# A three-stage attention and expert kernel: reductions through a transposing DMA, a capped work list, and scales from ScalarE's sums

## The chip, the cores and the metric

The kernel runs on one core of one Trainium2 chip. The metric is the device time of one execution in microseconds. Before the change it is 1496.46 us, the median of three runs (1494.01 to 1498.49). Engines are named as in the profile: PE is TensorE (PEld its weight loads), DVE is VectorE, ACT is ScalarE, POOL is GpSimd, and SP issues most DMAs.

## The reference

Three computations follow each other. The first is attention over 2 batches, 8 heads, 768 positions and 64 channels, in which a query sees only keys of its own cluster. The second is a network on its output, the third a mixture of 8 experts.

```python
# x: 1536 x 512, from the attention
h = x @ w_in                       # 512 x 2048
g = h * clip(h + 3.0, 0.0, 6.0) / 6.0
x = g @ w_out                      # 2048 x 512
logits = x @ w_gate;  logits = logits - logits.max()
P = exp(logits)
for _ in range(8):                 # balance rows and columns
    P /= P.sum(1) + 1e-09;  P /= P.sum(0) + 1e-09;  P *= N / E
out = 0
for e in range(8):
    out += P[:, e:e+1] * (maximum(x @ w1[e], 0.0) @ w2[e])    # 512 x 1024, 1024 x 512
```

## The kernel before

All matrix products work on pairs of float16 matrices: a float32 operand is scaled by a power of two and split into a high and a low part (names `ws`, `w_s`, `wop`, `xop`, `hh` and `hl`), and three products make one. The power of two comes from the largest absolute value of the operand. So for each operand that is split there is a maximum over a whole tile, and after it one scale.

Such a maximum is taken in two ways. `top_steps` writes each partition's maximum into a column of `pad` (DVE, L101), turns that column into rows by a matmul with the identity (PE, L77), reduces the rows on DVE (L82), and brings the result to all partitions by another matmul (PE, L87). `top_turned` (from L118) does without PE: DVE reduces, copies the maximum to a 128x128 block (L123), SP issues a transposing DMA (L124), and DVE reduces the turned block (L128). After both, `scale_of` makes the scale in four small operations of DVE (L140 to L149). Before the change `top_turned` serves the experts' weights from w1 of expert 1 and w2 of expert 0 on.

The work around the change has four parts. Every engine does its instructions in the order in which the program lists them, so an instruction that waits holds up all behind it on its engine.

1. Layer 1 of the first half of the network (`l1_mm`, L914 to L916) is 24 steps of twelve matmuls: 8 columns of hidden units, 3 blocks of 512 tokens. ACT and DVE make the activation from each step's result (L1231, L1232, L1238). Beside it DVE and ACT decode the second weights of this half (`w_1_c`, from L179) and split them (L271, L274).
2. Layer 2 of this half (L1260) is 24 steps of twelve matmuls, with ACT taking out each block (L1268). Beside it the weights of the second half are decoded: w_in (w1_0 of the task list, tiles `w_0_c`), the gate's weights (wg), and w_out (w1_1, tiles `w_1_c`). The order of a decode is load (L179), ACT L185, DVE L190 to L208, and a maximum by DVE L260 or by a sum of ACT L257.
3. The loop over the second half has 26 steps: layer 1 of a step, its activation, and layer 2 (L1260) of the step before the last one. After each block of 8 steps DVE adds four tiles of result into `acc` (L1270). At the end of each step `run_todo` runs some of a work list, `todo`: w1 of expert 0 in four pairs (`pair`, with POOL L1372 to L1378, ACT L1389 and DVE L1393, through one buffer `cmb`), the maximum of w2 of expert 0, and the splitting of the network's output, `x2_tasks`, for each finished block (x2_0, x2_1; x2_2 comes with the first units). A task's first number is its weight in the list; `run_todo` spends in a step the sum of weights divided by the steps left.
4. The experts are 96 units of 7 slots. Each slot has a product (L1660) and two groups of the second product (L1602), with ACT and DVE between them (L1561, L1566, L1665 to L1671). Weights of the next expert are loaded (L1417 for w2), their maxima taken (DVE L1422) and split (ACT L1389 and L1432) in between.

Of the kernel before, what the change touches and what calls it, by code (L numbers as in the profile page):

```python
# [9 lines left out]
F16 = mybir.dt.float16  # L10
# [22 lines left out]
def attention_moe_kernel(  # L33
# [82 lines left out]
    def top_turned(cols, name, then):  # L116

        pb = pad.bitcast(BF16)  # L118

        def a():  # L120
            m1 = small.tile([P, 1], F32, tag="w_m1", name=f"{name}_m1")
            nc.vector.tensor_reduce(m1, cols(), axis=AX.X, op=ALU.max)
            nc.vector.tensor_copy(pb[:, 0:P], m1.bitcast(BF16)[:, 1:2].to_broadcast([P, P]))  # L123
            nc.sync.dma_start_transpose(out=pad.bitcast(F16)[:, P:2 * P], in_=pad.bitcast(F16)[:, 0:P])  # L124

        def b():
            m = small.tile([P, 1], F32, tag="w_m", name=f"{name}_m")
            nc.vector.tensor_reduce(m, pb[:, P:2 * P], axis=AX.X, op=ALU.max)  # L128
            then(m)

        return [a, b]
# [86 lines left out]
    def weight_tasks(n, m, pool, raw=None):  # L218
# [70 lines left out]
        parts = []  # L289
        for i in range(NP):  # L290
            parts += [(0.05, lambda i=i: hi(i)), (0.2, lambda i=i: lo_pool(i)) if (n, m) == (1, 0) else (0.7, lambda i=i: lo(i))]
        scale = top_steps(lambda: d["mx"], 1, nm, room1, scale1)
        return start, [("m", piece(i)) for i in range(NP)], scale, parts

    def pipeline(pieces, depth):
# [704 lines left out]

    todo = []

    def run_todo(left):

        due = sum(c for c, _ in todo) / left
        while todo and (due > 0.01 or left <= 1):
            c, f = todo.pop(0)
            due -= c
            f()
            if f in far and left > 1:  # L1010
                return
# [3 lines left out]
    def turns(n):  # L1015
        def pause():
            pass

        far.append(pause)
        return [(0.0, pause)] * n  # L1020
# [16 lines left out]
    def gate_weights():  # L1037
        raw = mp.tile([P, KD, NE], F32, name="wg_raw")
        mx = small.tile([P, 1], F32, name="wg_mx")

        def g0():
            nc.sync.dma_start(raw, w_gate.rearrange("(c p) e -> p c e", p=P))

        def g1():
            nc.vector.tensor_reduce(mx, raw, axis=AX.XY, op=ALU.max, apply_absolute_value=True)

        def g1s(m):
            wgs["s"], wgs["i"] = scale_of(m, 1, 2, "wg", const)

        def g2():  # L1050
            nc.scalar.activation(wg[:, 0], raw, AF.Copy, scale=wgs["s"])
            nc.vector.scalar_tensor_tensor(
                out=wg[:, 1], in0=raw, scalar=wgs["s"], in1=wg[:, 0], op0=ALU.mult, op1=ALU.subtract)

        return [(0.05, g0), (0.3, g1)] + hops(top_steps(lambda: mx, 0, "wg", room1, g1s)) + [(0.3, g2)]

    cfac = {}

# [16 lines left out]
    xTf = xT.rearrange("p z c t n -> p (z c t n)")  # L1075
    XOP = 2 * 7 * 2 * XT

    def x2_tasks(bk, room):
        d = {}

        def q(h, g):
# [71 lines left out]
        vs = {"b12": q12, B11: q11, B21: q21, B22: q22, T1: T1, T2: T2, T3: T3, T4: T4}  # L1153
        t = [(0.9, lambda h=h, g=g: amax(h, g)) for h in range(2) for g in range(2)]
        t += [(0.1, diff(T1, q12, q11))]
        first, top, t = t, top_steps(lambda: d["mx"], 0, f"x2_{bk}", room, sc1), []
        order = [B11, B21, T1, B22, T2, "b12", T4, T3]
        for i, o in enumerate(order):
            t.append((0.1, hi(o, vs[o])))
# [11 lines left out]
    def balance_tasks():  # L1171
# [34 lines left out]
                o, i = (x.rearrange("p (g t) e -> p g t e", g=B)[:, :, NX * bk:NX * bk + NX, :] for x in (px, pr))  # L1206
                nc.vector.tensor_scalar(out=o, in0=i, scalar1=invx[bk][:, 0:1], scalar2=None, op0=ALU.mult)

        return top_steps(lambda: lg, 0, "lg", spare, m1) + [f for n in range(8) for f in (total, lambda n=n: col(n < 7))]

    coef = {}

# [38 lines left out]
    def layer2(n, blk, f):  # L1251
# [18 lines left out]
                nc.vector.scalar_tensor_tensor(  # L1270
                    out=o, in0=v, scalar=cfac[1], in1=o, op0=ALU.mult, op1=ALU.add)
        if n == 1:
            first, top, rest, logits = x2_tasks(blk, room1 if blk < NBK - 1 else spare)
            if blk < NBK - 1:
                todo[0:0] = first + hops(top, 1) + rest + turns(2) + [(0.5, lambda: logits(red_bank[-1]))]
            else:
                x2_last.extend((first, top, rest, logits))

# [62 lines left out]
    def expert_w1(e):  # L1341
# [22 lines left out]
        def pair(i):  # L1364
# [26 lines left out]
            def lo(k):  # L1391
# [6 lines left out]

        return (
            [lambda i=i: load(i) for i in range(4)], [lambda i=i: amax(i) for i in range(4)],  # L1400
            top_turned(lambda: d["mx"], f"w{n}_0", scale1) if e else top_steps(
                lambda: d["mx"], 1, f"w{n}_0", room1, scale1),
            [pair(i) for i in range(4)])

    def expert_w2(e):
# [13 lines left out]
                w2[e].rearrange("(a f p) n -> a p f n", a=2, p=P)[a, :, :, 256 * b:256 * b + 256])  # L1419

        def amax(j):
            nc.vector.tensor_reduce(  # L1422
                d["mx"][:, j:j + 1], rawbuf[:, j], axis=AX.X, op=ALU.max, apply_absolute_value=True)

        def scale1(m1):
            d["s"], wsc[n, 1] = scale_of(m1, 1, 3, "ws1", small, bufs=4)

        def src(k):
            return (R11, R21, R11, d.get("t1"), R12, R22, R21)[k]
# [40 lines left out]
    for s in range(len(steps) + LAG2):  # L1470
# [8 lines left out]
        if s == 4:  # L1479
            load, mx, sc, prs = expert_w1(0)  # L1480
            todo += [(0.05, f) for f in load] + [(6.0, nothing)] + [(1.2, f) for f in mx] + hops(sc)
            for c0, c1, hi, lo in prs:
                todo += [(0.1, c0), (0.1, c1), (0.1, hi[0]), (0.9, lambda hi=hi, lo=lo: (lo[0](), hi[1]()))]
                todo += [(0.4, lambda hi=hi, lo=lo: (lo[1](), hi[2]())), (1.3, lo[2])]
            load, mx, sc, hi, lo, ts = first_w2
            todo += [(0.05, f) for f in load] + [(6.0, nothing)] + [(1.2, f) for f in mx] + hops(sc)
        near = [(NB * f + blk) % 4 for _, blk, f in steps[max(0, s - 1):s + 2]]
        red_bank.append(BANKS[4 + next(b for b in range(4) if b not in near)])

        run_todo(max(2 if s + 1 < len(steps) + LAG2 else 1, len(steps) - 5 - s))  # L1490
    hctx.close()
    wctx.close()

# [218 lines left out]
    first, top, rest, logits = x2_last  # L1712
    for n, (_, f) in enumerate(first):
        at2(n, f)
    at_hops(5, top)
    for n, (_, f) in enumerate(rest):
        at2(9 + n, f)
    at2(9 + len(rest) + 2, lambda: logits(1))
# [59 lines left out]
```

## Time and profile before

| | us |
|---|---|
| median of three runs | 1496.46 (1494.01 to 1498.49) |
| the profiled execution | 1495.44, its span 1493.5 |
| busy in the span: PE, DVE, ACT, POOL | 1368.7, 1238.9, 873.1, 818.7 |
| layer 2 of the second half begins | 439.49 |
| the experts' main part | 690 to 1460 |

A busy time is the sum over an engine's instructions in the span. PE is the fullest one, with 92%, and its waits are gathered in a few places. The stretches that matter here are 338 to 353 (layer 1), 431 to 440 (the seam between the halves), 440 to 577 (the loop) and 577 to 690 (the first units).

### The profile page before, as it was taken

How to read it: one execution, taken by the hardware profiler on the slowest of the kernel's cores; microseconds unless marked ns; L12 is line 12 of the kernel's file. 1: busy time of each engine (PE TensorE's matmuls, PEld its weight loads, DVE VectorE, ACT ScalarE, POOL GpSimd, SP SyncE). 2: the span in 40 equal slices, each digit the busy share in tenths (PEclk: the TensorE clock that was granted, in tenths of full speed). 3: DMA queues.
4: the chain of work that ended last, by engine and by line, in shares of the span. 5: the costliest groups of instructions: out<-in, count | busy, mean ns of one | idle time of the engine just before them, and what ended most of it. 6: DMA issues, size and time to landing. Idle time of an engine off the chain costs nothing.

```text
span 1493.5 us, 31114 instructions
## 1 busy us (share of the span) xinstructions
PE 1368.7 (92%) x12361; PEld 1064.7 (71%) x12361; DVE 1238.9 (83%) x2154; ACT 873.1 (58%) x1636; POOL 818.7 (55%) x865
## 2 busy tenths in 40 slices
PE   2888788797999969799999999999999999999998
PEld 1556566543444425687888888888888888888887
DVE  7889998875775567999889989989989989989854
ACT  3568767566372444656667656656656656655642
POOL 1579888944121123845746646655655655655631
PEclk9789889998999989999999999999999999999999
DMA  8575743241420000101111011011011111111001
GB/s 222 140 159 102 153 83 70 60 127 39 127 88 27 29 28 2 43 16 43 31 45 48 26 44 58 16 44 58 23 37 58 31 31 57 31 30 58 9 29 50
DMA packets 148753, 88.62 MB, mean 59 GB/s; under 512 B 82048, under 2 KB 144512, under 8 KB 148608
## 3 DMA queue, kind: packets, MB, share of 16 engines
q1 hardware_dynamic: 148608, 86.64, 22.2%
q8 instruction: 96, 1.57, 0.4%
q14 instruction: 49, 0.40, 0.1%
HBM read 64.01 MB, written 3.15 MB: 45 GB/s over the span
## 4 chain that ended last, share of the span: by engine, by line
PE 69%; DVE 18%; ACT 4%; issue 4%; POOL 1%; DMA 1%; SPq 0%; DVEq 0%; ACTq 0%; POOLq 0%
PE o_X L1602 16%; PE X L1660 16%; PE o_Z L1602 8%; PE Z L1660 8%; PE Y L1660 4%; PE o_Y L1602 4%; DVE pmt L677 3%; PE l L1260 3%; PE l L914 2%; PE l L916 2%; PE l L915 2%; PE pmt L674 1%; DVE g L1566 1%; DVE raw L208 1%; DVE w_t L206 1%
## 5 line engine op out<-in xcount | busy, mean ns | idle before, releaser
L1660 PEld LDWEIGHTS <-wop 128*128 128x128 f16 x4032 | 395.5, 98 | 64.9 <-issue 17.9
L1602 PEld LDWEIGHTS <-g 128*128 128x128 f16 x4032 | 395.1, 98 | 46.2 <-DVE g L1566 0.3
L1602 PE MATMUL o_X<-ws,g 128*128 128x256 f16 x2304 | 312.1, 273 | 0.0
L1570 POOL TENSOR_TENSOR xT<-xT 128x256 f32<-128x256 f32 x96 | 77.6, 809 | 283.4 <-ACT xT L1671 283.4
L744 POOL TENSOR_TENSOR El<-E,Eh 128x384 f16<-128x384 f32 x192 | 189.8, 1017 | 72.6 <-DVE Eh L740 40.6
L1566 DVE TENSOR_TENSOR g<-xT,g 128x512 f16<-128x512 f32 (+1 forms) x288 | 225.5, 783 | 0.2
L1660 PE MATMUL X<-xop,wop 128*128 128x256 f16 x1536 | 210.2, 274 | 8.2 <-DVE xT L1668 4.7
L1561 ACT CAST g<-xT 128x512 f16<-128x512 f32 (+1 forms) x288 | 157.8, 548 | 2.8 <-POOL xT L1574 2.8
L1602 PE MATMUL o_Z<-ws,g 128*128 128x256 f16 x1152 | 157.2, 274 | 0.0
L1665 ACT COPY xT<-X 128x256 f32<-128x256 f32 x192 | 71.3, 372 | 146.4 <-PE X L1660 146.4
L731 ACT ACTIVATE E<-pS,esc 128x768 f32<-128x768 f32 x96 | 86.2, 900 | 65.5 <-PE pS L727 42.7
L1671 ACT ACTIVATE xT<-xT 128x256 f32<-128x256 f32 x192 | 100.1, 521 | 27.3 <-DVE xT L1668 27.0
L1671 ACT ACTIVATE xT<-X 128x256 f32<-128x256 f32 x96 | 36.8, 383 | 134.1 <-PE X L1660 133.9
L1660 PE MATMUL Z<-xop,wop 128*128 128x256 f16 x768 | 105.4, 274 | 5.4 <-ACT xT L1665 3.8
L1660 PE MATMUL X<-xT,wop 128*128 128x256 f16 x768 | 105.4, 274 | 0.8 <-DVE xT L1668 0.8
L1630 DVE SCALAR_TENSOR_TENSOR acc<-o_X,coef,acc 128x256 f32<-128x256 f32 x168 | 73.0, 475 | 28.1 <-PE o_X L1602 28.1
L677 DVE TENSOR_REDUCE pmt<-pmt 128x1 f32<-128x768 f32 x84 | 80.5, 959 | 18.9 <-PE pmt L674 18.3
L1574 POOL TENSOR_TENSOR xT<-xT 128x256 f32<-128x256 f32 x96 | 93.1, 970 | 0.0
L674 PE MATMUL pmt<-kA,qA 80*128 80x384 f16 x184 | 51.7, 367 | 43.2 <-DVE pmt L677 13.8
L1575 POOL TENSOR_TENSOR sb<-xT 128x256 f32<-128x256 f32 x96 | 86.8, 904 | 7.5
L1571 POOL TENSOR_TENSOR sb<-xT 128x256 f32<-128x256 f32 x96 | 82.5, 860 | 5.0 <-ACT xT L1665 4.3
L1435 DVE SCALAR_TENSOR_TENSOR ws<-raw,ws_s,ws 128x1024 f16<-128x1024 f32 x48 | 80.8, 1684 | 0.9 <-ACT ws L1432 0.9
(304 smaller groups left out, 2900.7 us busy)
## 6 DMA issues: line engine op xcount, KB each, us to landing
raw<-in_moe_w_dram SPq DMA_DIRECT2D x64, 256.0 KB, 3.2
raw<-in_moe_w_dram SPq DMA_DIRECT2D x32, 512.0 KB, 3.5
w_c<-in_moe_w_out_dram SPq DMA_DIRECT2D x16, 512.0 KB, 3.3
w00x<-in_moe_w_in_dram SPq DMA_DIRECT2D x8, 512.0 KB, 5.2
w00f<-in_moe_w_in_dram SPq DMA_DIRECT2D x8, 512.0 KB, 4.4
w_c<-in_moe_w_in_dram SPq DMA_DIRECT2D x8, 512.0 KB, 3.9
qraw<-in_q_dram SPq DMA_DIRECT2D x8, 384.0 KB, 3.9
kraw<-in_k_dram SPq DMA_DIRECT2D x8, 384.0 KB, 4.8
```

The source lines that it names most:

```text
L677: nc.vector.tensor_reduce(nmx[i][:, j:j + 1], ps[:, :, 0:N2], axis=AX.XY, op=ALU.max, negate=True)
L731: nc.scalar.activation(E, ps[:, :, 0:N2], AF.Exp, scale=d["esc"][:, 0:1])
L744: nc.gpsimd.tensor_tensor(out=El[:, g], in0=E[:, g], in1=Eh[:, g], op=ALU.subtract)
L1435: nc.vector.scalar_tensor_tensor(out=w2op[k][:, 1], in0=src(k), scalar=d["s"][:, 0:1], in1=w2op[k][:, 0], op0=ALU.mult, op1=ALU.subtract)
L1561: nc.scalar.copy(t[:, 0] if n == 2 else t[:, 0, 0], src)
L1566: nc.vector.tensor_tensor(o, d[g], x, op=ALU.subtract)
L1571: nc.gpsimd.tensor_tensor(out=d["sb"][:, 0], in0=q3, in1=q2, op=ALU.subtract)
L1574: nc.gpsimd.tensor_tensor(out=sa[:, 0], in0=sa[:, 1], in1=q3, op=ALU.subtract)
L1575: nc.gpsimd.tensor_tensor(out=d["sb"][:, 1], in0=q1, in1=sa[:, 0], op=ALU.subtract)
L1602: nc.tensor.matmul(o, lhsT=x, rhs=r, start=first and z == 0, stop=last and z == 2, skip_group_check=True)
L1660: nc.tensor.matmul(o[n][:, 0:XT], lhsT=l, rhs=r, start=(first and c == 0 and z == 0), stop=(c == 1 and z == 2), skip_group_check=True)
L1671: nc.scalar.activation(q, q if src is None else src, AF.Relu)
```

## The change

It has three parts. First, nine maxima go from `top_steps` to `top_turned`: the weights w0_1, w1_0, wg and w1_1 of the network, w1 of expert 0, the three blocks x2 and the logits lg. Second, the last loop's work list is spent with a cap of 3.2 per step, only the last step empties it, x2 tasks go to its end in place of its front, and the last two parts of a pair are a turn apart. Third, from expert 1 on the scale of w2 comes from a sum of absolute values on ACT and a target of 13, in place of a maximum on DVE and a target of 3.

```diff
@@ top_turned
         def a():
             m1 = small.tile([P, 1], F32, tag="w_m1", name=f"{name}_m1")
-            nc.vector.tensor_reduce(m1, cols(), axis=AX.X, op=ALU.max)
+            x = cols()
+            nc.vector.tensor_reduce(m1, x, axis=AX.X if len(x.shape) == 2 else AX.XY, op=ALU.max)
...
@@ weight_tasks (w0_1, w1_0, w1_1)
-        scale = top_steps(lambda: d["mx"], 1, nm, room1, scale1)
+        scale = top_turned(lambda: d["mx"], nm, scale1)
...
-    def run_todo(left):
-
-        due = sum(c for c, _ in todo) / left
+    def run_todo(left, most=1e9):
+
+        due = min(sum(c for c, _ in todo) / left, most) if left > 1 else 0
         while todo and (due > 0.01 or left <= 1):
             c, f = todo.pop(0)
             due -= c
...
-        return [(0.05, g0), (0.3, g1)] + hops(top_steps(lambda: mx, 0, "wg", room1, g1s)) + [(0.3, g2)]
+        return [(0.05, g0), (0.3, g1)] + hops(top_turned(lambda: mx, "wg", g1s)) + [(0.3, g2)]
...
-        first, top, t = t, top_steps(lambda: d["mx"], 0, f"x2_{bk}", room, sc1), []
+        first, top, t = t, top_turned(lambda: d["mx"], f"x2_{bk}", sc1), []
...
-        return top_steps(lambda: lg, 0, "lg", spare, m1) + [f for n in range(8) for f in (total, lambda n=n: col(n < 7))]
+        return top_turned(lambda: lg, "lg", m1) + [idle] + [f for n in range(8) for f in (total, lambda n=n: col(n < 7))]
...
             if blk < NBK - 1:
-                todo[0:0] = first + hops(top, 1) + rest + turns(2) + [(0.5, lambda: logits(red_bank[-1]))]
+                todo.extend(first + hops(top, 1) + rest + turns(2) + [(0.5, lambda: logits(red_bank[-1]))])
...
-            top_turned(lambda: d["mx"], f"w{n}_0", scale1) if e else top_steps(
-                lambda: d["mx"], 1, f"w{n}_0", room1, scale1),
+            top_turned(lambda: d["mx"], f"w{n}_0", scale1),
...
         def amax(j):
-            nc.vector.tensor_reduce(
-                d["mx"][:, j:j + 1], rawbuf[:, j], axis=AX.X, op=ALU.max, apply_absolute_value=True)
+            if e == 0:
+                nc.vector.tensor_reduce(
+                    d["mx"][:, j:j + 1], rawbuf[:, j], axis=AX.X, op=ALU.max, apply_absolute_value=True)
+                return
+            junk = epool.tile([P, 1024], F16, tag="ev", name=f"w{n}_1_t{j}", bufs=3)
+            nc.scalar.activation(junk, rawbuf[:, j], AF.Abs, accum_out=d["mx"][:, j:j + 1])
 
         def scale1(m1):
-            d["s"], wsc[n, 1] = scale_of(m1, 1, 3, "ws1", small, bufs=4)
+            d["s"], wsc[n, 1] = scale_of(m1, 1, 13 if e else 3, "ws1", small, bufs=4)
...
-                todo += [(0.4, lambda hi=hi, lo=lo: (lo[1](), hi[2]())), (1.3, lo[2])]
+                todo += [(0.4, lo[1])] + turns(1) + [(0.1, hi[2]), (1.3, lo[2])]
...
-        run_todo(max(2 if s + 1 < len(steps) + LAG2 else 1, len(steps) - 5 - s))
+        run_todo(2 if s + 1 < len(steps) + LAG2 else 1, 3.2)
...
-    at_hops(5, top)
+    at_hops(5, top, 4)
```

After the change most lines have a number higher by one (L915 is L914 of before, L1394 is L1393, L125 is L124); from the new sum on it is four.

The first place is PE in layer 1 of the first half, at the maximum of w0_1. Before:

```order
L916 MATMUL l_0_2_5_5310<-xT,w_0_s 128x512
L77 MATMUL red_5330<-ident,pad 128x128
L87 MATMUL red_5334<-ident,w_1_r 128x1
L914 LDWEIGHTS w_0_s
L914 MATMUL l_0_0_6_5342<-xT,w_0_s 128x512
```

At the same place after:

```order
L917 LDWEIGHTS w_0_s
L917 MATMUL l_0_2_5_5313<-xT,w_0_s 128x512
L915 LDWEIGHTS w_0_s
L915 MATMUL l_0_0_6_5341<-xT,w_0_s 128x512
L916 LDWEIGHTS w_0_s
```

The two matmuls of the maximum are gone from PE's row; the layer's matmuls follow each other.

The second place is SP's queue before the loads of the second half's w_out (`w_1_c`), with the gate's weights ahead of them. Before:

```order
L179 DMA w_0_c_5593<-in_moe_w_in_dram 128x1024
L179 DMA w_0_c_5614<-in_moe_w_in_dram 128x1024
L1042 DMA wg_raw<-in_moe_w_gate_dram 128x4x8
L179 DMA w_1_c_5752<-in_moe_w_out_dram 128x1024
L179 DMA w_1_c_5754<-in_moe_w_out_dram 128x1024
L179 DMA w_1_c_5756<-in_moe_w_out_dram 128x1024
```

After:

```order
L180 DMA w_0_c_5592<-in_moe_w_in_dram 128x1024
L180 DMA w_0_c_5613<-in_moe_w_in_dram 128x1024
L1043 DMA wg_raw<-in_moe_w_gate_dram 128x4x8
L125 DMA_TRANSPOSE pad<-pad 128x128 x2
L180 DMA w_1_c_5749<-in_moe_w_out_dram 128x1024
L180 DMA w_1_c_5751<-in_moe_w_out_dram 128x1024
```

Two transposes, those of w1_0 and wg, now stand ahead of the eight loads.

The third place is DVE in the last loop, ahead of the evacuation of a block (`acc`), with the pairs of expert 0's w1 (`wop`, their last part from `cmb`). Before, at the second block:

```order
L1393 SCALAR_TENSOR_TENSOR wop_2_6678<-raw,ws_s,wop_2_6678 128x512
L1232 SCALAR_TENSOR_TENSOR u_2_0_6695<-u_2_0_6695,l_1_2_0_6682 128x512
L1239 TENSOR_TENSOR hl_2_0_6699<-u_2_0_6695,hh_2_0_6698 128x512
L1393 SCALAR_TENSOR_TENSOR wop_2_6678<-raw,ws_s,wop_2_6678 128x256
L1393 SCALAR_TENSOR_TENSOR wop_2_6678<-cmb_2_6673,ws_s,wop_2_6678 128x1024
L1393 SCALAR_TENSOR_TENSOR wop_3_6722<-raw,ws_s,wop_3_6722 128x512
L1393 SCALAR_TENSOR_TENSOR wop_3_6722<-raw,ws_s,wop_3_6722 128x256
L1393 SCALAR_TENSOR_TENSOR wop_3_6722<-cmb_3_6717,ws_s,wop_3_6722 128x1024
L1232 SCALAR_TENSOR_TENSOR u_2_1_6747<-u_2_1_6747,l_1_2_1_6734 128x512
L1239 TENSOR_TENSOR hl_2_1_6751<-u_2_1_6747,hh_2_1_6750 128x512
L1270 SCALAR_TENSOR_TENSOR acc<-l_1_1_0_6407,cfac_6023,acc 128x2x256
```

After, at the first block, where the pairs now stand:

```order
L1394 SCALAR_TENSOR_TENSOR wop_0_6303<-raw,ws_s,wop_0_6303 128x512
L1394 SCALAR_TENSOR_TENSOR wop_0_6303<-raw,ws_s,wop_0_6303 128x256
L1233 SCALAR_TENSOR_TENSOR u_1_0_6321<-u_1_0_6321,l_1_1_0_6308 128x512
L1240 TENSOR_TENSOR hl_1_0_6325<-u_1_0_6321,hh_1_0_6324 128x512
L1394 SCALAR_TENSOR_TENSOR wop_0_6303<-cmb_0_6298,ws_s,wop_0_6303 128x1024
L1394 SCALAR_TENSOR_TENSOR wop_1_6347<-raw,ws_s,wop_1_6347 128x512
L1394 SCALAR_TENSOR_TENSOR wop_1_6347<-raw,ws_s,wop_1_6347 128x256
L1233 SCALAR_TENSOR_TENSOR u_1_1_6365<-u_1_1_6365,l_1_1_1_6352 128x512
L1240 TENSOR_TENSOR hl_1_1_6369<-u_1_1_6365,hh_1_1_6368 128x512
L1271 SCALAR_TENSOR_TENSOR acc<-l_1_0_0_6089,cfac_6019,acc 128x2x256
```

Two pairs' `cmb` rows stood between two u before; now there is at most one, and u and hl stand between a pair's raw rows and its `cmb` row.

## Rows read from the trace of the kernel before

**Rows 1.** Busy time by stretch: stretch, length, engines, PE clock, DMA.

```profile
338.00:353.00 15.00, 6.99 (x22) 2.78 (x21) 7.33 (x17) 8.00 (x15) 8.02 (x6) 0.66 0.23 70
353.00:369.50 16.50, 16.50 (x78) 7.51 (x77) 8.68 (x14) 12.93 (x20) 7.04 (x6) 1.00 0.00 1
439.50:576.60 137.10, 123.35 (x614) 56.06 (x613) 84.90 (x137) 53.63 (x81) 25.46 (x25) 0.95 0.10 31
525.00:541.00 16.00, 5.15 (x15) 1.74 (x13) 11.07 (x17) 5.27 (x7) 7.23 (x7) 0.68 0.19 66
577.00:690.00 113.00, 95.11 (x834) 79.95 (x832) 105.25 (x200) 66.57 (x140) 70.84 (x68) 0.96 0.10 30
690.00:1460.00 770.00, 767.18 (x7019) 686.63 (x7018) 679.71 (x1147) 467.29 (x979) 452.55 (x488) 1.00 0.12 38
```

**Rows 2.** Timeline, PE at 343 us: start, duration, idle before and releaser.

```profile
343.94 0.45 PE L77 MATMUL red<-ident,pad 128*128 128x128 f32 x1 [4.47 <-DVE pad L101]
347.93 0.59 PE L87 MATMUL red<-ident,w_r 128*128 128x1 f32 x2 [3.54 <-DVE w_r L82]
348.38 0.59 PE L914 MATMUL l<-xT,w_s 128*128 128x512 f16 x1
352.17 0.58 PE L914 MATMUL l<-xT,w_s 128*128 128x512 f16 x1
```

**Rows 3.** Tile pad, steps of top_turned: count, min/median/max ns; the transpose's landing.

```profile
L123 DVE COPY pad<-w_m x15: 226/568/570, 568.7 to 1379.7; 128x128 bf16<-128x128 bf16 x15
L124 SPq DMA_TRANSPOSE pad<-pad x15: 1094/1095/1827, 569.0 to 1380.2; - x15
L128 DVE TENSOR_REDUCE w_m<-pad x15: 271/274/281, 572.1 to 1385.6; 128x1 f32<-128x128 bf16 x15
DMA to landing us min/median/max: 2.2/2.3/2.9
```

**Rows 4.** Timeline of the decode and the seam; last, landing of L179.

```profile
394.60 0.16 DVE L101 TENSOR_REDUCE pad<-w_mx 128x1 f32<-128x8 f32 x1
399.50 0.16 DVE L140 TENSOR_SCALAR wg_e<-red 128x1 int32<-128x1 int32 x1 [0.47 <-PE red L87]
403.72 0.94 DVE L190 TENSOR_SCALAR w_t<-w_t 128x512 f32<-128x512 f32 x1 [3.04 <-ACT w_t L185]
...
432.35 0.14 DVE L149 TENSOR_SCALAR ws_s<-ws_e 128x1 int32<-128x1 int32 x1
434.56 0.78 ACT L1231 ACTIVATE u<-l,three,hinv 128x512 f32<-128x512 f32 x1 [3.27 <-PE l L916]
436.74 0.69 DVE L1239 TENSOR_TENSOR hl<-u,hh 128x512 f16<-128x512 f32 x1 [0.68 <-ACT hh L1238]
439.49 0.38 PE L1260 MATMUL l<-hh,w_s 128*128 128x512 f16 x1
...
DMA to landing us min/median/max: 3.2/4.0/6.0
```

**Rows 5.** Chain of waits and timeline in the last loop.

```profile
465.55 2.59 PE l L1260 x12
...
531.11 1.15 ACT L1389 ACTIVATE wop<-cmb,ws_s 128x1024 f16<-128x1024 f32 x1 [3.93 <-POOL cmb L1378]
536.27 0.61 PE L1260 MATMUL l<-hh,w_s 128*128 128x512 f16 x1 [10.85 <-DVE acc L1270]
```

**Rows 6.** PE's waits, 440 to 577 and 690 to 1494: total, times, longest.

```profile
PE red L87 <- DVE x_r L82: 2.4, 2, 1.8
...
PE X L1660 <- DVE xT L1668: 2.8, 6, 0.5
```

**Rows 7.** Maximum and sum: groups of lines L1422 and L257; ACT's timeline.

```profile
L1422 DVE TENSOR_REDUCE w_mx<-raw 128x1 f32<-128x1024 f32 x27 | 32.6, 1207 | 0.0
...
L257 ACT ACTIVATION_READ_ACCUMULATOR w_t<-raw x16: 185/187/188, 311.9 to 428.8; 128x1 f32 x16
...
907.20 0.38 ACT L1671 ACTIVATE xT<-X 128x256 f32<-128x256 f32 x1 [1.19 <-PE X L1660]
```

More of the change, by code (lines that the diff above doesn't have):

```diff
@@ L1076, in attention_moe_kernel, with x2_tasks @@
     XOP = 2 * 7 * 2 * XT
-    def x2_tasks(bk, room):
+    def x2_tasks(bk):
         d = {}
@@ L1272, in layer2 @@
         if n == 1:
-            first, top, rest, logits = x2_tasks(blk, room1 if blk < NBK - 1 else spare)
+            first, top, rest, logits = x2_tasks(blk)
             if blk < NBK - 1:
-                todo[0:0] = first + hops(top, 1) + rest + turns(2) + [(0.5, lambda: logits(red_bank[-1]))]
+                todo.extend(first + hops(top, 1) + rest + turns(2) + [(0.5, lambda: logits(red_bank[-1]))])
             else:
```

## The prediction

> **What bounds the kernel now.** PE does by far the most work on this core, so a gain has to shorten a stretch in which PE is short of work. The table of busy times by stretch says which, and I read it first [rows 1]; then the timeline in the holes, for what PE waited for; then the sums of waits, for what is left elsewhere. From 690 to 1460 us PE is busy 767.18 of 770 us. Against that it works 6.99 of 15 us at 338 to 353, 5.15 of 16 at 525 to 541, and 95.11 of 113 at 577 to 690, where DVE is the fuller engine with 105.25. The change touches these three holes and the seam between the two networks' halves at 431 to 440; the long expert part can give next to nothing.
>
> **A and B: the maxima leave PE's queue, and the seam.** In the hole at 343 us the timeline shows the mechanism [rows 2]. The matmul of L77 waits 4.47 us for DVE's row maximum, the one of L87 3.54 us for the next maximum, and all layer-1 matmuls stand behind them in PE's order though they need neither. PE then runs at the lower of its two levels (granted 0.66 over the stretch): nine intervals between L914 rows every third matmul, from 348.38 to 352.17, hold nine matmuls in 3.79 us, 0.42 each, where the network's full-speed group takes 2.59 / 12 = 0.216 [rows 5]. About ten such matmuls lose 2.1 us. In the changed order no reduction matmul stands there, so PE's layer 1 ends 4.47 + 3.54 + 2.1 = 10.1 us earlier.
>
> Not all of this arrives. The next bound is the decode of the second weights on DVE and ACT. ACT is busy 12.93 of the 16.5 us after 353 [rows 1], so its tail can move up by some of the 10.1 us and not all: I take 6.7. The decode chain then has three of the turned maxima in it (w1_0, wg, w1_1), on which DVE waits directly. One of them takes a copy of 0.57, a landing of 2.3 and a reduction of 0.27 us, 3.1 in all [rows 3], and 3.3 with the reduction ahead of the copy (0.16, the row at 394.60). The first two took 399.50 - 394.60 = 4.9 us with the first one's scale between them [rows 4]; now it is 2 x 3.3 and about 0.6 for that scale, 7.2: 2.3 us later. A second cost is on SP: the eight L179 loads of the second w_out half stand behind both transposes. The wg copy ends at 394.60 - 6.7 + 3.3 + 0.6 + 0.73 = 392.5, SP issues its transpose in 1.1 us [rows 3], and the first load needs 3.2 to 6.0 (median 4.0) to land [rows 4]: 397 to 400, against the first use by ACT, which I expect at 398.8 (DVE's row at 403.72 less 4.4, and 0.6 for ACT's step ahead of it). I book 0.1 us there. The third maximum costs 0.5. So the last scale, ready at 432.35 + 0.14, moves by 6.7 - 2.3 - 0.1 - 0.5 = 3.8 us, to 428.7.
>
> At the seam something else moved the end. ACT's u(0) at 434.56 waited 3.27 us for PE, not for the scale, because PE's three leading layer-1 steps of the second half stood behind the last L87; they also fill the time up to 439.49 [rows 4]. Now they start when layer 2 ends, some 10 us sooner, and are done before the scale is there. u(0) follows the scale at 428.8; from u(0) to the end of hl were 436.74 + 0.69 - 434.56 = 2.9 us, and one weight row of 0.7 lies behind it: layer 2 begins at 432.4 instead of 439.49, 7.1 us sooner. PE idles before that and will run its first group at the lower level, as it did after 348 us: minus 2.1. **A and B together: 5.0 us** (1 to 8; the low end is a decode chain that eats the shift, the high end one in which the loads are early and the clock stays up).
>
> **C: the last loop.** From 439.5 to the end of its last group it takes 137.1 us [rows 1]. The work in it is 45 groups of twelve matmuls (24 + 24, less the three leading ones) at 2.59 [rows 5], 116.6, and for the small logit matmuls I add 1: 117.6. The difference of 19.5 us is the hole of 10.85 at 536.27 [rows 5], waits of 2.4 for L87 [rows 6], the reduction matmuls themselves, and the lower clock behind each hole (0.68 at 525 to 541; 0.95 over the loop). The hole is no lack of DVE time, since DVE is busy 11.07 of those 16 us; it is the order. One expert weight pair goes POOL → ACT → DVE through a single cmb buffer: ACT waits 3.93 us for it [rows 5] and then works 1.15 on it and about as long on the two raw blocks beside it, so I put the cycle at 6.2 us. Two or more such pairs stand on DVE ahead of the four acc evacuations of the block, and PE needs their banks at once. In the new order one pair stands per step, and each pair's cmb row comes a step after the raw ones, behind u and hl, so that POOL and ACT have a step's time for it. A step is 5.18 us and a pair 6.2, so the four pairs slip by some 3 to 4 us together; hl of a step has about a step and a half until its use, so it bears that. The acc evacuations have less: bank 0 must be free 2.59 us after the block's last matmul, hl ends some 0.6 after it (2.9 from u, which starts 2.59 before), and an evacuation of 128x512 takes 0.69 as hl does [rows 4], which leaves some 1.3 us. At the first boundary only one pair is ahead of it, at the second two x2 rows. I therefore take the whole 19.5 (13 to 20: the low end is a repeat of half the hole plus its clock).
>
> **D: the step into the experts.** x2_1 now runs in the last six steps, its last rows and the logits come behind the last acc evacuations on DVE, and unit 0 needs the bank of these logits. DVE bounds 577 to 690, so what is pushed in there counts: about 2.4 us (three rows of 0.7 and a copy for lg), less one L1422 of 1.21 [rows 7]: **+1.2 us** (-3, if the freed reductions and the direct waits for Z and X weigh more, to +6, if the x2_1 rows lag a whole step).
>
> **E: the w2 scales.** 28 reductions of 1.207 us leave DVE [rows 7], 33.8 us of work. But PE waited for DVE only 2.8 us after 690 [rows 6], in six waits, so at most 2.8 comes back. I take 1.5. ACT gets 28 sums of 128x1024: an activation of that shape takes 1.15 [rows 5], the reading of a sum 0.19 [rows 7]; as the activation's row covers part of the reading, 1.24 is my estimate, 1.15 to 1.34 its bounds. What hides them is ACT's idle time before the relu of the next product: 1.19 us at 907.20, in a unit with one weight row [rows 7]. That is just covered, with some slack in the g casts; without the cover 28 x 1.24 = 34.7 us would be on the path.
>
> **Sum.** 1495.44 (the profiled execution: span 1493.5 and 1.9 around it) - 5.0 - 19.5 + 1.2 - 1.5 = 1470.6. The median of the three runs is 1.0 above that execution: 1471.6; I say 1471.
>
> **A rule against it.** The trace has the chip's transposing DMA at 2.3 us to landing [rows 3] and PE's own transposing matmul at about 0.45 [rows 2]. The Trainium skill, VectorE: DVE Perf Modes, section "The three transpose paths", gives TensorE 390 ns and the DMA 1309 ns for 128x128, and its section "Rules for kernel authors" wants TensorE for it where PSUM will do. By its figures the nine moved maxima would cost 9 x 0.92 = 8.3 us more (an estimate from that page), and the sum would be 1479. The trace agrees with the direction of these prices, with 2.3 as the landing; it doesn't agree that they decide, since PE stood 8.0 us for one maximum.
>
> **The rivals.**
> R1, the decode chain swallows A and B. For it: SP's loads behind two waiting transposes, with landings up to 6.0. Against it: decode uses one load per 2.3 us of DVE work or more, and buffers run ahead. They are 0: 1476. Chance 0.13.
> R2, the pacing doesn't do what it says: DVE is late at a block boundary and the hole forms again. For it: 6.2 per pair against 5.18 per step, and 1.3 us of slack at the banks. C is 19.5 - 10.85 = 8.7: 1482. Chance 0.13.
> R3, slower: the sums fall on PE's path. ACT's casts g and relus feed PE; if each of 28 sums delays a unit by its 1.24 us, 34.7 us are added: 1506. It decides over the rest from 24.8 / 28 = 0.89 us a sum. Against it: idle 1.19 us at that place, and no PE wait for ACT after 690. Chance 0.04.
> R4, the round trip on the path: each of nine maxima costs DVE or its customer 2.0 us more (3.3 less 0.45 and 0.59 for the two matmuls [rows 2] and 0.27 for a reduction between them), 18 us: 1489. Against it: for six of them other work stands between. Chance 0.04. This is the mechanism by which the page's rule would hold.
> R5, more than forecast: the decode shift arrives whole, or DVE's relief makes 577 to 690 shorter by 3 us or more: 1463 to 1466. Chance 0.1.
> The forecast, 1467 to 1475, has the remaining 0.56.
>
> **Numbers.** From R5 to a little beyond R2 holds over 8 in 10: 1462 to 1485. About 0.3%, 4.5 us, is what a measurement of this kernel can tell from nothing. Only R3 and mishaps beyond R4 end over 1492: faster 0.92, same 0.04, slower 0.04.
>
> **What would show it.** After: no matmul wait over 1 us between 338 and 353, and granted clock 1.0 there; ACT's u(0) of the second half about 6 us before 434.56 while PE waits some 7 us at the seam; in the last loop no PE wait for acc over 2 us, and a loop of about 118 us; 577 to 690 no shorter; after 690 PE waits under 2 us in total and none for ACT. It is wrong if PE waits anew at the two block boundaries, if SP's loads land after 400 on the old scale, or if ACT appears among PE's releasers in the experts.

## The result and the profile after

The changed kernel takes 1481.34 us, the median of four runs (1478.91 to 1482.32), against 1496.3 for the kernel before: a ratio of 0.9894, with a 95% interval of 0.9877 to 0.991 (the two medians alone give 0.9900). A later series of the same kernel gave 1477.72 us and 0.9867 (0.9845 to 0.9889). The profiled execution has 1478.91 us and a span of 1477.0.

Four points in the program cut the span into the stretches of the forecast. They are read from the views of single lines of code, in which a row ends in the first and the last start of its group. Before:

```profile
L914 PE MATMUL l<-xT,w_s x96: 377/379/634, 290.3 to 365.3; 128*128 128x512 f16 x96
...
L1260 PEld LDWEIGHTS <-w_s x288: 97/98/152, 439.3 to 576.4; 128*128 128x128 f16 x144
...
L1660 PEld LDWEIGHTS <-wop x4032: 95/98/181, 576.6 to 1469.3; 128*128 128x128 f16 x192
L1660 PE MATMUL X<-xT,wop x768: 269/273/421, 651.0 to 1469.4; 128*128 128x256 f16 x192
...
L1602 PE MATMUL o_X<-ws,g x2304: 269/273/282, 609.1 to 1489.1; 128*128 128x256 f16 x192
```

After:

```profile
L915 PE MATMUL l<-xT,w_s x96: 377/379/379, 292.8 to 356.7; 128*128 128x512 f16 x96
...
L1261 PEld LDWEIGHTS <-w_s x288: 97/98/151, 432.9 to 554.6; 128*128 128x128 f16 x144
...
L1664 PEld LDWEIGHTS <-wop x4032: 95/98/152, 555.8 to 1452.9; 128*128 128x128 f16 x192
L1664 PE MATMUL X<-xT,wop x768: 269/273/273, 636.6 to 1453.0; 128*128 128x256 f16 x192
...
L1606 PE MATMUL o_X<-ws,g x2304: 269/273/283, 592.3 to 1472.6; 128*128 128x256 f16 x192
```

Layer 1 starts at 290.3 before and at 292.8 after, though the attention ahead of it is the same code; over the 13 profiled executions of this study that start lies between 288.8 and 295.1. So a single execution says nothing finer than some 3 us about the whole, and the comparison goes from this point on. "A and B" is from it to the first layer-2 weights of the second half, "C" from there to the first expert product, "D" on to the first product of the third block (`X<-xT`), "E" on to the last `o_X`.

| us | forecast of the change | before | after | measured |
|---|---|---|---|---|
| A and B | -5.0, of it +2.1 for the clock in C | 149.0 | 140.1 | -8.9 |
| C | -19.5 | 137.3 | 122.9 | -14.4 |
| D | +1.2 | 74.4 | 80.8 | +6.4 |
| E | -1.5 | 838.1 | 836.0 | -2.1 |
| sum | -24.8 | 1198.8 | 1179.8 | -19.0 |

The whole times of these two executions differ by 16.5 us (1495.44 and 1478.91); the 2.5 us between that and 19.0 is the later start of layer 1.

The stretch table of after, with the columns of [rows 1]:

```profile
343.00:353.00 10.00, 10.00 (x48) 4.52 (x47) 6.64 (x17) 7.70 (x14) 6.18 (x5) 1.00 0.38 126
432.90:440.00 7.10, 7.07 (x21) 2.57 (x22) 5.73 (x9) 5.50 (x9) 1.78 (x3) 0.61 0.39 116
440.00:554.80 114.80, 112.89 (x552) 51.53 (x551) 80.14 (x131) 48.53 (x74) 25.62 (x22) 1.00 0.10 31
555.80:592.30 36.50, 25.02 (x190) 19.35 (x187) 31.98 (x49) 20.69 (x45) 26.56 (x22) 0.86 0.01 2
592.30:636.60 44.30, 38.94 (x359) 33.12 (x357) 40.72 (x79) 24.62 (x53) 21.54 (x20) 0.96 0.17 49
675.60:1444.00 768.40, 765.59 (x7007) 685.32 (x7005) 656.38 (x1113) 494.00 (x1031) 460.70 (x488) 1.00 0.12 38
```

Layer 1 no longer has a hole: PE is busy all of 343 to 353, at a granted clock of 1.00 where it was 0.66. The loop has lost its second hole too, and PE works 112.89 of 114.8 us in it; but its first 7 us run at 0.61. In the two stretches after 555.8 PE still idles, 11.5 and 5.4 us, while DVE is busy 31.98 of 36.5 and 40.72 of 44.3.

PE's waits after, in three windows (280 to 440, 440 to 577 and 675 to 1480), answer to [rows 6]:

```profile
PE l L1261 <- ACT w_s L272: 5.5, 1, 5.5
...
PE X L1664 <- DVE lg L1150: 2.6, 1, 2.6
PE l L915 <- DVE u L1233: 1.9, 1, 1.9
...
PE X L1664 <- DVE xT L1672: 2.8, 6, 0.5
```

No wait is left for a maximum, nor for acc. Three new ones stand in their place: 5.5 us at the seam, 1.9 in the loop, 2.6 at unit 0. The last row, the experts', is word for word the wait of before, 2.8 us in six pieces.

The decode of the second half's weights and the seam, from the timeline (start, duration, engine; in brackets the idle time before and its releaser):

```profile
390.13 0.16 DVE L123 TENSOR_REDUCE w_m<-w_mx 128x1 f32<-128x8 f32 x1
396.75 0.15 DVE L141 TENSOR_SCALAR wg_e<-wg_m 128x1 int32<-128x1 int32 x1
...
426.50 0.23 DVE L124 COPY pad<-w_m 128x128 bf16<-128x128 bf16 x1
426.76 1.09 SPq L125 DMA_TRANSPOSE pad<-pad  x1
429.01 0.29 DVE L129 TENSOR_REDUCE w_m<-pad 128x1 f32<-128x128 bf16 x1 [2.28 <-DMA pad<-pad]
429.77 0.14 DVE L150 TENSOR_SCALAR ws_s<-ws_e 128x1 int32<-128x1 int32 x1
430.10 0.78 ACT L1232 ACTIVATE u<-l,three,hinv 128x512 f32<-128x512 f32 x1 [1.51 <-DVE hinv L1062]
432.16 1.33 ACT L272 ACTIVATE w_s<-raw,ws_s 128x512 f16<-128x512 f32 x2
432.93 0.61 PE L1261 MATMUL l<-hh,w_s 128*128 128x512 f16 x1 [5.47 <-ACT w_s L272]
```

The last maximum's copy starts at 426.50, its transpose lands 2.28 us after, and the scale is ready at 429.91. ACT's u(0) then waits for it (1.51 us) and no more for PE as in [rows 4]. PE waits 5.47 us, and starts layer 2 at 432.93 at the lower clock.

### The profile page after: what moved, and what is told of

Read it like the earlier page. It is cut to its first block, busy times and chain, and to the rows that moved or that the text cites. A ratio compares the mean times of both kernels' runs of the same rounds, so it can differ in the third digit from the quotient of the medians.

```text
span 1477.0 us, 31136 instructions
## 1 busy us (share of the span) xinstructions
PE 1363.5 (92%) x12334; PEld 1062.7 (72%) x12334; DVE 1219.2 (83%) x2135; ACT 900.6 (61%) x1692; POOL 827.7 (56%) x865
## 4 chain that ended last, share of the span: by engine, by line
PE 67%; DVE 20%; ACT 4%; issue 4%; DMA 1%; POOL 1%; SPq 0%; DVEq 0%; ACTq 0%; POOLq 0%
PE o_X L1606 16%; PE X L1664 16%; PE o_Z L1606 8%; PE Z L1664 8%; PE Y L1664 4%; PE o_Y L1606 4%; DVE pmt L678 3%; PE l L1261 2%; PE pmt L675 2%; PE pv L760 1%; DVE raw L209 1%; DVE g L1570 1%; DVE w_t L207 1%; ACT u L1232 1%; PE pS L728 1%
## 5 line engine op out<-in xcount | busy, mean ns | idle before, releaser
L1570 DVE TENSOR_TENSOR g<-xT,g 128x512 f16<-128x512 f32 (+1 forms) x288 | 234.0, 813 | 0.2
L1579 POOL TENSOR_TENSOR sb<-xT 128x256 f32<-128x256 f32 x96 | 90.1, 939 | 7.5
L1575 POOL TENSOR_TENSOR sb<-xT 128x256 f32<-128x256 f32 x96 | 85.8, 894 | 5.0 <-ACT xT L1669 4.3
L1373 POOL TENSOR_TENSOR cmb<-raw 128x256 f32<-128x256 f32 x32 | 25.0, 783 | 102.2 <-DVE wop L1394 83.5
```

The costliest lines, as they stand in the source:

```text
L1570: nc.vector.tensor_tensor(o, d[g], x, op=ALU.subtract)
L1575: nc.gpsimd.tensor_tensor(out=d["sb"][:, 0], in0=q3, in1=q2, op=ALU.subtract)
L1579: nc.gpsimd.tensor_tensor(out=d["sb"][:, 1], in0=q1, in1=sa[:, 0], op=ALU.subtract)
```

## The experiments

All are given with the stretches of the table, each from one profiled execution. Each ratio is to the kernel before, run in the same series; its median there was 1495.6 for e1 to e3, 1499.5 for e4 to e7 (this series has no run of the changed kernel), and 1496.3 for e8 to e11. So across series the ratios are to be compared, not the medians.

| us | median | ratio to before | A and B | C | D | E |
|---|---|---|---|---|---|---|
| before | 1496 | 1 | 149.0 | 137.3 | 74.4 | 838.1 |
| after | 1481.3 | 0.9894 [0.9877, 0.991] | 140.1 | 122.9 | 80.8 | 836.0 |
| after again (e8) | 1477.7 | 0.9867 [0.9845, 0.9889] | 140.3 | 122.6 | 83.6 | 836.1 |
| e1 maxima only | 1488.1 | 0.9952 [0.9935, 0.9969] | 140.8 | 133.3 | 78.4 | 837.8 |
| e2 pacing only | 1487.2 | 0.9949 [0.9933, 0.9966] | 149.2 | 125.3 | 78.2 | 836.4 |
| e3 sums only | 1495.9 | 1.0004 [0.9993, 1.0015] | 148.6 | 137.3 | 74.5 | 838.0 |
| e4 after, logits in unit 0 | 1477.0 | 0.9856 [0.9834, 0.9879] | 140.2 | 122.0 | 81.0 | 836.1 |
| e5 after, balance later | 1473.2 | 0.9834 [0.9805, 0.9862] | 140.1 | 122.6 | 77.1 | 837.9 |
| e6 after, two maxima on PE | 1479.7 | 0.9879 [0.9855, 0.9903] | 143.2 | 120.4 | 82.5 | 835.2 |
| e7 after, sums for w2 of expert 0 | 1481.2 | 0.9881 [0.9854, 0.9907] | 140.3 | 121.5 | 81.4 | 837.8 |
| e9 e5 and sums for w1 | 1472.1 | 0.9837 [0.9818, 0.9856] | 140.0 | 122.3 | 74.1 | 837.7 |
| e10 e5 and e4 | 1470.8 | 0.9829 [0.9811, 0.9847] | 140.1 | 121.3 | 74.5 | 837.9 |
| e11 all three | 1469.9 | 0.9816 [0.9798, 0.9835] | 141.1 | 122.0 | 74.2 | 836.0 |

### The three parts alone: e1, e2, e3

e1 is the kernel before with the first part of the change: all its lines with `top_turned`.

```diff
-        scale = top_steps(lambda: d["mx"], 1, nm, room1, scale1)
+        scale = top_turned(lambda: d["mx"], nm, scale1)
...
-    at_hops(5, top)
+    at_hops(5, top, 4)
```

Expected: 

> Before, with the nine maxima moved to the transposing DMA and nothing else changed. Theory (the maxima pay by leaving PE's queue): the 8 us of waits at 343 us and the seam give about 9 us, less 2 for the lower clock at the seam; in the last loop the waits for L87 (2.4 and 0.5) and their matmuls go, 3 to 4 us; the hole of 10.85 us at the second block boundary stays. Time 1484 to 1488. Rival (the hole in the loop came from the maxima standing between the tasks): the hole goes too and the time is 1476 or less.

e2 is the kernel before with the second part.

```diff
-                todo[0:0] = first + hops(top, 1) + rest + turns(2) + [(0.5, lambda: logits(red_bank[-1]))]
+                todo.extend(first + hops(top, 1) + rest + turns(2) + [(0.5, lambda: logits(red_bank[-1]))])
...
-        run_todo(max(2 if s + 1 < len(steps) + LAG2 else 1, len(steps) - 5 - s))
+        run_todo(2 if s + 1 < len(steps) + LAG2 else 1, 3.2)
```

Expected: 

> Before, with the work list capped at 3.2 a step and in its new order, maxima and scales as before. Theory (the hole is the order alone): PE's wait of 10.85 us for acc goes with the low clock behind it, 12 to 13 us, the waits for L87 stay, and the step into the experts costs 3 to 5 us more, as unit 0 waits for the logits' bank: 1487 to 1489. Rival (the pacing costs as much at the end as it gives): 1494 to 1497.

e3 is the kernel before with the third part.

```diff
+            nc.scalar.activation(junk, rawbuf[:, j], AF.Abs, accum_out=d["mx"][:, j:j + 1])
...
-            d["s"], wsc[n, 1] = scale_of(m1, 1, 3, "ws1", small, bufs=4)
+            d["s"], wsc[n, 1] = scale_of(m1, 1, 13 if e else 3, "ws1", small, bufs=4)
```

Expected: 

> Before, with only the w2 scales from expert 1 on taken from ScalarE's sums. Theory (nothing of DVE's relief reaches PE after 690 us): within 1 us of before, and PE's waits after 690 are still about 2.8 us in six. First rival, the forecast's term: 1.5 us faster. Second rival, sums on PE's path: up to 35 us slower, with PE waiting for ACT.

Measured: 1488.06, 1487.23 and 1495.85 us; in each case the theory's side. PE's waits from 440 to 577, first of e1, then of e2:

```profile
PE l L1261 <- DVE acc L1271: 10.9, 1, 10.9
```

```profile
PE X L1660 <- DVE lg L1149: 2.2, 1, 2.2
PE l L914 <- DVE u L1232: 2.0, 1, 2.0
PE red L87 <- DVE x_r L82: 1.1, 2, 0.5
```

With the maxima alone the hole at the block boundary is still there (10.9 us, against 10.85 before [rows 5]); with the pacing alone it is gone, and the small waits of the maxima are left. So the hole was the old order and pacing of the work list (e2's cap, new order and shifted pair parts were not run one by one), and A and B were the maxima: e1 has nearly the whole gain of A and B (140.8 against 140.1), e2 none of it. e2 also shows the price of the pacing, 2.2 us of wait for lg at unit 0 and 2.0 for u in the loop, which the other parts have nothing to do with. And e1 has a price in D that the forecast did not name: 78.4 against 74.4, without the new order of the list; e5 shows below where it comes from. The parts add up: 0.48, 0.51 and -0.04% make 0.95, each known to within 0.1 to 0.2; the whole gave 1.06 and 1.33.

e3 settles E: 1.0004 (0.9993 to 1.0015). The sum fits under ACT's wait, as one of them shows in the timeline of after (ACT):

```profile
889.50 1.05 ACT L1427 ACTIVATE w_t<-raw 128x1024 f16<-128x1024 f32 x1
890.45 0.19 ACT L1427 ACTIVATION_READ_ACCUMULATOR w_t<-raw 128x1 f32 x1
890.79 0.38 ACT L1675 ACTIVATE xT<-X 128x256 f32<-128x256 f32 x1 [0.15 <-PE X L1664]
```

Activation and reading take 890.64 - 889.50 = 1.14 us together, and of the idle time before the relu, 1.19 [rows 7], 0.15 is left. DVE loses 28 reductions of 1.2 us, 33.8 us in all, but its busy time falls by only 23 (656 us of 675 to 1444, against 680 of 690 to 1460 before): some of its other rows got longer, as the product rows `g<-xT` 128x512, from 889 to 925 ns each. PE gets none of it.

### The step into the experts: e4, e5

e4 puts the second block's logit matmuls behind unit 0's second product, into a bank that unit 0's products don't use.

```diff
-                todo.extend(first + hops(top, 1) + rest + turns(2) + [(0.5, lambda: logits(red_bank[-1]))])
+                todo.extend(first + hops(top, 1) + rest + turns(2) + [
+                    (0.5, (lambda: logits(red_bank[-1])) if blk == 0 else (lambda: x2_mid.append(logits)))])
...
+    at2(1, lambda: x2_mid[0](0, True))
+    at2(2, logits_outs[1])
```

Expected: 

> The changed kernel (1481.3), with the logit matmuls of the second block moved behind unit 0's second product and into another bank. Theory (unit 0 waits 2.6 us for DVE's lg, and PE runs the first products at the lower clock after that): the wait is gone and 2.5 to 4 us with it, 1477.5 to 1479. Rival (DVE, not the bank, sets the pace of the first units): PE waits for xT instead and the time is within 1 us of 1481.

Measured: 1476.99 us. The wait for lg is gone, but D is 81.0 against 80.8 and 83.6 in the two executions of after, and C is 0.6 to 0.9 shorter by the matmuls that moved out of it. In place of lg PE waits longer for xT, as the rival had it, here between 555 and 690 (after has 5.1 us in four waits in that row, e8 5.7):

```profile
PE X L1674 <- DVE xT L1682: 6.5, 5, 2.4
```

By its time alone it looks like the theory's gain; after's own second series (1477.7) shows that such a difference is no proof. The trace speaks for the rival; the time decides nothing by itself.

e5 puts the balance chain back to where it began before the change.

```diff
-    at_hops(9 + len(rest) + 5, balance_tasks(), 5)
+    at_hops(9 + len(rest) + 10, balance_tasks(), 5)
```

Expected: 

> The changed kernel with the balance chain five slots later, where it stood before the change. Theory (the chain, starting five slots sooner, meets the w2 splits on DVE and makes PE wait 2.4 us more for xT at the units around 618 to 640): 1.5 to 3 us less, 1478.5 to 1480. Rival (the chain's work only moves, DVE has the same sum of work): within 1 us of 1481.

Measured: 1473.23 us, and D is 77.1, against 80.8 and 83.6. `top_turned` has two steps and an idle one where `top_steps` has five, so with the same first slot the chain behind the logits' maximum comes five slots sooner, onto DVE's splits of w2. From after's timeline (DVE, then PE):

```profile
608.11 0.27 DVE L129 TENSOR_REDUCE lg_m<-pad 128x1 f32<-128x128 bf16 x1
609.01 0.25 DVE L1185 TENSOR_REDUCE b_rs<-pr 128x12 f32<-128x96 f32 x1 [0.44 <-ACT pr L1180]
610.06 0.32 DVE L1190 TENSOR_REDUCE b_cs<-pr 128x8 f32<-128x96 f32 x1
610.30 1.28 DVE L1439 SCALAR_TENSOR_TENSOR ws<-raw,ws_s,ws 128x1024 f16<-128x1024 f32 x1
611.50 0.42 DVE L1672 TENSOR_TENSOR xT<-X,xT 128x256 f32<-128x256 f32 x1
611.97 0.97 PE L1664 MATMUL X<-xop,wop 128*128 128x256 f16 x6 [2.38 <-DVE xT L1672]
```

The first balance round (609.01 to 610.38) stands ahead of a split (L1439, 1.28 us), both ahead of the small addition that PE needs, and PE waits 2.38 us for it. In e5 this wait isn't there; PE's waits of 555 to 690, first after, then e5:

```profile
PE X L1664 <- DVE xT L1672: 5.1, 4, 2.4
PE Y L92 <- DVE xT L1672: 2.6, 2, 2.0
```

```profile
PE X L1664 <- DVE xT L1672: 3.3, 3, 1.8
PE Y L92 <- DVE xT L1672: 2.0, 1, 2.0
```

The largest single wait falls from 2.4 to 1.8 and the sum from 5.1 to 3.3; the wait for lg stays at 2.6. e1, which has the earlier chain too, has the same wait of 2.38 us for xT, at 618.61. The rival, that the chain's work only moves, is not borne out: E is 1.9 longer than in after's profile, but the whole from layer 1 to the end is still 2.1 us shorter (1177.7 against 1179.8, and 1182.6 in e8). The time itself, 5 us below the theory's range, proves less: its ratio is clear of after's first series but overlaps that of e8. What carries the reading is that all four versions with the later chain (e5, e9 to e11) take 1173.3 to 1177.7 us from layer 1 to the end, and all five of the changed kernel with the earlier one (after, e4, e6, e7, e8) 1179.3 to 1182.6.

### The transposing DMA against PE where DVE waits directly: e6

e6 takes two of the maxima in the decode chain, w1_0 and wg, back to PE; the line for wg is shown, the one for w1_0 changes alike.

```diff
-        return [(0.05, g0), (0.3, g1)] + hops(top_turned(lambda: mx, "wg", g1s)) + [(0.3, g2)]
+        return [(0.05, g0), (0.3, g1)] + hops(top_steps(lambda: mx, 0, "wg", room1, g1s)) + [(0.3, g2)]
```

Expected: 

> The changed kernel with the maxima of w1_0 and wg back on PE's matmuls, where DVE waits directly behind each. Theory (there the round trip through SP is the slower one: from the first reduction to the scale of wg 4.9 us by PE and 6.6 by the DMA): the decode chain and the seam come 1.5 to 2 us sooner, 1479 to 1480, with no new wait of PE at the seam. Rival (PE's waits of about 1 us in layer 2 and the lower clock cost as much): within 1 us of 1481, or slower.

Measured: 1479.7 us. The time lies in the theory's range, but the theory fell: the seam is 3.1 us later, not sooner (A and B 143.2). From e6's timeline (PE and DVE):

```profile
390.45 0.45 PE L77 MATMUL red<-ident,pad 128*128 128x128 f32 x1 [4.34 <-issue]
396.55 0.27 PE L77 MATMUL red<-ident,pad 128*128 128x128 f32 x1
396.86 0.29 DVE L82 TENSOR_REDUCE wg_r<-red 128x1 f32<-128x128 f32 x1 [4.30 <-PE red L77]
398.08 0.14 DVE L150 TENSOR_SCALAR wg_s<-wg_e 128x1 int32<-128x1 int32 x1
...
431.37 0.78 ACT L1233 ACTIVATE u<-l,three,hinv 128x512 f32<-128x512 f32 x1 [1.94 <-PE l L918]
436.30 0.38 PE L1262 MATMUL l<-hh,w_s 128*128 128x512 f16 x1
```

PE, 10 us earlier in its order than before, now stands at L77 for 4.34 us (the profile puts it down to issue; DVE's row maximum ended at 390.35), and the second maximum's matmul lies behind twelve layer-2 matmuls that take 4.60 us at a granted clock of 0.51, so DVE waits 4.30 us for it. The scale of wg is done at 398.2 where it was 397.3 in after. That 0.9 us is not what moved the seam. PE's own queue is: with 4.34 us of waiting and the lower clock behind it, PE reaches its three leading layer-1 steps so late that ACT's u(0) waits 1.94 us for them, and PE starts layer 2 at 436.30 straight behind them, with no idle time, where it stood 5.47 us in after. The DMA costs 2.3 us each time; PE's price depends on what stands ahead of it in its queue. What the seam lost, C got back: 120.4, the shortest of all, since no lower clock follows at its start (granted clock 1.00 over 436 to 445, where after has 0.61 from 432.9).

### One step of the loop: e7

e7 takes the scale of expert 0's w2 from ScalarE's sums too, with the target of 13.

```diff
-            if e == 0:
-                nc.vector.tensor_reduce(
-                    d["mx"][:, j:j + 1], rawbuf[:, j], axis=AX.X, op=ALU.max, apply_absolute_value=True)
-                return
```

Expected: 

> The changed kernel with the scale of expert 0's w2 also from ScalarE's sums, in the last loop. Theory (three maxima of 1.2 us in one step make DVE late and PE waits 1.9 us for u at 507): the wait is gone, 1479 to 1480. Rival (the lateness comes from the x maxima and the pairs): the wait stays above 1 us and the time within 1 us of 1481.

Measured: 1481.18 us. The wait for u is 0.9 instead of 1.9 us and C 121.5, 1.4 shorter than after's, but from layer 1 to the end e7 takes 1181.0 us, between the two executions of after (1179.8 and 1182.6). So half of the wait was the w2 maxima's, the other half stayed, and the time followed the rival. What made DVE late is seen in after (DVE, then PE):

```profile
494.97 3.46 DVE L1423 TENSOR_REDUCE w_mx<-raw 128x1 f32<-128x1024 f32 x3
498.36 0.67 DVE L1233 SCALAR_TENSOR_TENSOR u<-u,l 128x512 f32<-128x512 f32 x1
...
505.13 1.86 DVE L1088 TENSOR_REDUCE x_mx<-acc 128x1 f32<-128x512 f32 x3
506.91 0.68 DVE L1233 SCALAR_TENSOR_TENSOR u<-u,l 128x512 f32<-128x512 f32 x1
507.64 0.38 PE L915 MATMUL l<-xT,ws 128*128 128x512 f16 x1 [1.91 <-DVE u L1233]
```

Three maxima of w2 in one step hold back u by 3.46 us, two steps later three of x2_0 by 1.86, and at 507.64 PE has waited 1.91 us for that u to free its bank.

### Versions: e8 to e11

e8 is the changed kernel unchanged, to stand beside the others. e9 adds to e5 the sums for w1 from expert 1 on; e10 is e5 with e4; e11 has all.

```diff
+            junk = epool.tile([P, 1024], F16, tag="ev", name=f"w{n}_0_t{i}", bufs=3)
+            nc.scalar.activation(junk, rawbuf[:, i], AF.Abs, accum_out=d["mx"][:, i:i + 1])
...
-            d["s"], wsc[n, 0] = scale_of(m1, 1, 2, "ws0", small, bufs=4)
+            d["s"], wsc[n, 0] = scale_of(m1, 1, 12 if e else 2, "ws0", small, bufs=4)
```

Expected of e8: 

> The changed kernel once more, beside the three versions below: 1479 to 1483. From the start of the first half's layer 1 to the end 1180 us, the part before it 289 to 295, as it is the same code in all kernels and has moved between executions by that much.

Expected of e9: 

> The changed kernel with the balance chain five slots later and the maxima of the experts' w1 from expert 1 on taken as ScalarE's sums too. Theory (DVE sets the pace from 555 to 676, and four of these maxima of 1.21 us fall there): 2 us from the chain and 2 to 4 from the maxima, 1475 to 1478. Rival (DVE's relief reaches PE no more there than after 690): as with the chain alone, 1478 to 1480.

Expected of e10: 

> The changed kernel with the balance chain five slots later and the second block's logits inside unit 0. Theory by the trace of the version with the logits alone (its wait of 2.6 us went, but the downstream stretch only got 0.6 shorter): 1478 to 1479, no better than the chain alone by more than 1 us. Rival by its times (4.3 below the changed kernel): 1474 to 1476.

Expected of e11: 

> The changed kernel with all three: chain later, logits inside unit 0, sums for w1. Theory: 1474 to 1477, faster than the changed kernel. Rival (the three reliefs are one and the same stretch of DVE and do not add): 1477 to 1479.

Measured: 1477.72, 1472.11, 1470.75 and 1469.85 us. Each is below what its theory expected, by 1.3, 2.9, 7.3 and 4.2 us, e8 too, which is the changed kernel itself: by its two series that kernel is at 1478 to 1481. D falls to 74.1 to 74.5 in all three versions, the value of before, so the loss in D can be undone in two ways. They don't add: e11's D is 74.2. e10 is under even its rival's range: the logits' place, which alone changed little that the trace shows, takes D from e5's 77.1 to 74.5 once the chain is out of the way. e11 is 1.84% faster than the kernel before (1.65 to 2.02) and faster than the changed one: its interval, 0.9798 to 0.9835, lies below that of e8, 0.9845 to 0.9889, on the same chip.

## Why the prediction was right in the main, and where it was not

The direction and the places held, and the time fell inside the wide range, 1462 to 1485. It fell outside the forecast's own 1467 to 1475. The size was 15 us (18.6 in the second series) for 25. The first series ended at 1481, beside R2's 1482, without R2's hole: the neighbourhood is chance. In part the misses also cancelled: with the clock's 2.1 us counted in C for both, A and B gave 1.8 us more than forecast and E 0.6 more, C 3.0 less (3.2 from the forecast's own start, 137.1) and D 5.2 less.

Of the signs named ahead, layer 1 (no wait over 1 us, clock 1.00), no wait for acc and 577 to 690 no shorter came true. The loop took 122.9 us and not 118, and PE's waits after 690 are 2.8 us and not under 2.

**A and B, held and under-sized.** The chain of maxima began as forecast, at 390.13, which is 387.6 on the clock of before, 7.0 us sooner than 394.60 [rows 4] for 6.7. Its first two took 6.6 us to 396.75 and not 7.2, because the copy took 0.23 us and not 0.57. The forecast had the last scale at 428.7; it was ready at 429.91 with a layer 1 that began 2.5 us later, 427.4 on the old clock. The start of layer 2 came 8.9 us sooner, not 7.1. SP's loads behind the two transposes cost nothing: ACT waits for no w_out load in the decode. The lower clock at the seam came as expected (0.61 over 7.1 us). R1 did not happen.

**C, the step that failed is "hl of a step has about a step and a half until its use, so it bears that".** It counted the pairs alone, and it looked at the use of hl, while PE waited at the bank of layer 1 that u frees. The list also has four maxima of w2 in it, which the cap of 3.2 lets pass three at a time, and the maxima of x2. With them u was late and PE waited 1.9 us (e2 has it too, 2.0). That is 1.9 of the 3.2 us between 122.9 and the forecast's 119.7 (117.6 and 2.1 for the clock); of the other 1.3, 0.4 is the clock and 0.6 the logit matmuls. From 432.90 on, 21 matmuls took 7.07 us where 21 x 0.216 = 4.5, so the lower clock cost 2.5 (e6, without it, is 2.5 shorter); and the logit matmuls of a block take 0.8 us (556.68 to 557.49 in e4), for two blocks 1.6 where the forecast added 1; the last 0.3 is open. R2, a new hole at the block boundary, did not happen; e1 and e2 show that the old one came from the work list, not from the maxima.

**D, the term of +1.2 us was mis-sized, and in two ways.** The wait for lg's bank at unit 0 was seen coming, but priced as DVE work: PE stood 2.56 us from its last logit matmul, at 556.02, through the rest of DVE's acc rows (to 557.70), one x2 row of 0.73 and lg's 0.24. And a move went uncounted: the balance chain starts five slots sooner. e1 shows it without the pacing (+4.0), e5 takes it away (-3.7 from after's profile). D is +6.4 and +9.2 us in the two executions of after; the bound of +6 was too near.

**E, -1.5 was nothing.** e3 has no gain, and PE's waits after 690 are 2.8 or 2.9 us in six pieces in every version but e6 (2.4 in five), e3 included, so the w2 maxima were never what these waits were for. The 2.1 us by which E is shorter in after's profile also come and go between the versions (835.2 to 838.1, e5 and e10 nearly have the value of before); I leave their cause open. R3 stays out: a sum takes 1.14 us, ACT still waits 0.15 for PE behind it at the place shown, and no PE wait for ACT appears after 690.

**R4 and the page's rule.** e6 is the test: the Trainium skill, VectorE: DVE Perf Modes, section "Rules for kernel authors", prefers TensorE for a 128x128 transpose where PSUM will do. Here the two maxima on PE came out 3.1 us later at the seam, by the wait of 4.34 us in PE's own row and the lower clock behind it, and no faster in all; and e1, with all nine by the DMA, is 0.48% faster than the kernel before. The trace does not agree with the rule in this place.

## What to carry to other kernels

A reduction that borrows an engine with a long queue costs what stands in that queue, on both sides (8.0 us of PE for the maximum of w0_1 before, 4.30 of DVE in e6); a path of its own (2.3 us) can be the better one, though it is slower alone. When a helper gets fewer steps, everything scheduled after it moves, so count the slots of what follows, not only of what was edited. Work taken off an engine paid here only where another engine waited for it: 34 us of DVE reductions gave nothing after 690 us, while a small chain moved by five slots made D 3.7 us shorter and the whole 2.1 or more.

## What the runs showed of the hardware

The broadcast copy of 128x128 bf16 took 0.23 us in some places and 0.57 in others (0.226 to 0.572 in after, over 19 of them); I had priced it at 0.57 everywhere. After PE's 5.47 us of idle at 427 us the granted clock was 0.61 for the next 7 us, and 1.00 over the 115 us behind it. Identical code for the attention ended, by layer 1's first matmul, anywhere between 288.8 and 295.1 us.
